# Weight tiles kept in attention's resting K and V buffers, and the first K at the head of the queue

## The chip, the cores and the metric

The kernel runs on one core of a Trainium2 chip. Times are microseconds (us) of the device. The kernel before took 807.57 us, the median of three runs (807.21 to 809.88).

The engines are named as the profile names them: PE is the matrix engine, PEld its weight loads, DVE the vector engine, ACT the scalar engine, POOL the GpSimd engine, and SP the engine whose queue starts nearly all DMAs. SPq is SP's sequencer.

## The reference

Block-sparse attention over 4 batches, 8 heads, 768 positions and 64 features, then a feed-forward layer over all 3072 positions:

```python
scores = scale * np.matmul(q, k.transpose(0, 1, 3, 2))
mask = np.abs(blk_i - blk_j) <= 1                      # blocks of 32
mask = mask | (blk_i == 0) | (blk_j == 0) | (blk_i == n_blocks - 1) | (blk_j == n_blocks - 1)
for qb in range(n_blocks):
    for kb in sampled_blocks[qb]:                      # three sampled blocks for each
        mask[qb * block:(qb + 1) * block, kb * block:(kb + 1) * block] = True
attn = softmax(np.where(mask, scores, -1e9))
x = np.matmul(attn, v)                                 # -> (3072, 512)
h = x @ w_in                                           # (512, 2048)
return (h - np.tanh(h)) @ w_out                        # (2048, 512)
```

## The kernel before, in words

**Feed-forward units.** The 3072 tokens are six chunks of 512, the 2048 hidden features sixteen stripes of 128. A unit is one chunk with one stripe `ft`; there are 96 (`UNITS`). `first` makes h of the unit by 12 matmuls with the tile `wi` of the stripe, `bent` makes h - tanh(h) on ACT, DVE and POOL, and `second`, two units later, adds the stripe's part of the output by 12 matmuls with the tile `wo`. Weights and activations are split into a high and a low part (hence three products for each). A tile `wi` or `wo` is 128x1024 words, 512 KB, high half and low half.

**The order of the units** (`SEGS`): units 0 to 7 are chunk 0 with stripes 0 to 7, units 8 to 15 chunk 1 with stripes 0 to 7, units 16 to 23 chunk 1 with stripes 8 to 15, units 24 to 31 chunk 0 with stripes 8 to 15, and from unit 32 on a chunk at a time.

**How a weight tile is made.** The weights come as 64-bit words. `load` brings the raw words of a tile (512 KB) into one of three raw buffers (two tiles `rv` and `spare`), `convert` makes 32-bit numbers of them by three operations on DVE, by way of a PSUM bank, and `split` writes the high part (ACT) and the low part (POOL). `save` writes the finished tile to device memory (`w2i`, `w2o`), from which `get` brings it back for a later chunk. Tiles of stripes 0 to 2 stay on the chip; the others pass through rings of three tiles, `wi` and `wo`. The stripes of the first half are made before and during units 0 to 7, those of the second half during units 8 to 22, one each 0.94 units (`CONVB`). Their conversion passes through PSUM banks 6 and 7, which attention also uses.

**What `ahead` means.** A second-half tile that is made more than `AHEAD` = 2.2 units before its use is split in place: high and low part are written over the raw words. It is then saved, and fetched again by `get` for its unit among 16 to 23. All sixteen are such tiles. A raw buffer is free for the next load only when the save has read it.

**Attention.** It works in attention units of their own, each with one query block and half of the heads. Attention units 0 to 7 run before feed-forward unit 0, attention units 8 to 15 (for chunk 1) until about unit 8, and attention unit 16 starts near 22.7. For each, `gather_k` copies the K blocks that its queries see into `kr0` or `kr1` (on POOL; on DVE for the first two), `gather_v` brings the V rows into `vw00`, `vw01` or `vw10`, `vw11` by DMA, `scores` multiplies, and so on. `fresh` leaves out the blocks that a buffer still holds. `load_samples` reads the sampled block numbers and computes on DVE the offsets `kx` and `vx`, which the gathers read into registers. `ks` holds all of K, half 0 and half 1, four DMAs of 768 KB each (`load_k`).

**What sets the order.** Each step is put into a list with a time in units (`at`), the list is sorted, and each engine then runs its instructions in that order, SP its DMAs too. Nothing overtakes: a DMA that must wait on SP holds those behind it.

The lines that set the second half's order are these:

```python
ahead = ft >= HALF and ft + HALF + NEED[m] - t0 > AHEAD
at(max(t0 - 1.8, free[k - 3] if k > 2 else -99), self.load, m, ft, k)
at(end + 0.03, self.split, m, ft, ahead)
at(end + 0.4, self.save, m, ft)
free.append(end + (1.2 if ahead else 0.01))
at(max(u + g, sent[m, ft]), self.get, m, u)
```

Of the kernel before, what the change touches and what calls it, by code (L numbers as in the profile page):

```python
# [11 lines left out]
F32 = mybir.dt.float32  # L12
F32R = mybir.dt.float32r
# [28 lines left out]
STEPS = dict(w=0.5, t=0.61, hs=0.605, th=0.82, p1=0.83, qq=0.87, mk=0.97, p2=1.05, p3=1.27, cp=1.49, gh=1.78, gl=1.9)  # L42
GETI, GETO = -1.6, 1.0
NEED = {"i": -0.6, "o": 1.9}
AHEAD = 2.2
CHUNKS = [[4 * n + 1 + j for j in range(4)] for n in range(5)] + [[21, 22, 0, 23]]
HALF = NFT // 2
SEGS = [(0, 0, HALF), (1, 0, HALF), (1, HALF, NFT), (0, HALF, NFT)] + [(n, 0, NFT) for n in range(2, len(CHUNKS))]
# [99 lines left out]
class Attention:  # L148
    def __init__(self, tc, k, q, v, samp, rows, ffn, ident, banks, att, sm, f2, rv, at):
        self.tc, self.nc = tc, InOrder(tc)  # L150
        self.k, self.q, self.v, self.ffn, self.ident, self.banks = k, q, v, ffn, ident, banks
        self.sm, self.f2, self.att, self.rv = sm, f2, att, rv
        self.ks = att.tile([P, 2, H, S], F32, name="ks")
        self.vw = [[att.tile([P, B, VW], F32, name=f"vw{i}{x}") for x in range(2)] for i in range(2)]
        self.kr = [att.tile([P, H, 256], F32, name=f"kr{i}") for i in range(2)]
        self.kx, self.vx = (att.tile([1, 66], I32, name=f"{n}x") for n in "kv")
        self.held = {}
        self.vals, self.qs, self.ve = {}, {}, {}
        self.ms, self.nbs, self.ps, self.pts, self.nbe, self.es, self.wts = ({} for _ in range(7))
        self.kept = [ffn.spare.bitcast(F32)[:, 256 * i : 256 * i + 256] for i in range(3)]  # L160

        units = []
        last = {}

        def add(c, time, **kw):
            u = Unit(len(units), c, time, **kw)
            u.i, u.before = c, last.get(c)
            if u.n < LEAD - 2:
                u.i, u.before = u.n % 2, units[u.n - 2] if u.n > 1 else None
            elif u.n < LEAD:  # L170
                u.before = units[u.n - 2]
            if u.b:
                last[c] = u
            units.append(u)

        for c in range(2):
            for b in CHUNKS[0]:
                add(c, 0, b=b)
        for m, blocks in list(enumerate(CHUNKS))[1:]:
            steps = [(c, dict(b=b, quick=m < 3)) for b in blocks if 0 < b < NB - 1 for c in range(2)]  # L180
            edges = [(g // 2, dict(f=g % 2, k=k)) for g in EDGES.get(m, ()) for k in range(3)]
            steps += edges
            for i, (c, kw) in enumerate(steps):
                add(c, BAND[m][0] + BAND[m][1] * (i - 2 * (m == 1)), **kw)
        lead = lambda x: (x - T0) * RATE
        at(lead(-9), self.load_q, units[0])
        for bt in range(B):
            at(lead(-8.9), self.load_k, 0, bt)
        at(lead(-8.95), self.load_samples, samp, rows)
        for c, t in ((1, lead(-2.5)),):  # L190
            for bt in range(B):
                at(t, self.load_k, c, bt)
        for u in units:
            t, n = u.t, u.n
            if u.b:
                if n:
                    at(max(t["s"] - 2.0, units[n - NQ].t["s"] + 0.01) if n >= NQ else lead(-8.95 + 0.01 * n), self.load_q, u)
                at(max(t["s"] - 1.2, u.before.t["s"] + 0.01 if u.before else lead(-3)), self.gather_k, u)
                at(max(t["s"] - 2.0, u.before.t["pv"] + 0.01 if u.before else lead(-3)), self.gather_v, u)
            else:  # L200
                if u.k == 0:
                    at(units[n - 1].t["s"] + 0.02, self.load_q, u)
                at(units[n - 2].t["pv"] + 0.02, self.load_ve, u)
            at(t["s"], self.scores, u)
            at(t["m"], self.most, u)
            at(t["e1"], self.exps, u, 1)
            at(t["e0"], self.exps, u, 0)
            at(t["turn"], self.turn, u)
            at(t["c1"], self.copy, u, 1)
            at(t["c0"], self.copy, u, 0)  # L210
            at(t["pv"], self.accum, u)
            at(t["norm"], self.norm, u)
            if u.b:
                for x in "hl":
                    at(t["norm"] + (0.1 if x == "h" else 0.15), self.put, u, x)
            elif u.k == 2:
                at(t["e0"] + 0.12, self.weigh, u)
                end = 2 * u.c + u.f in EDGES[len(CHUNKS) - 1]
                quiet = iter([t["norm"] + 0.1 + 0.08 * j for j in range(6)] if end else self.quiet(units[u.n + 1 :], t["norm"]))
                for k in range(3):  # L220
                    for s in range(1 + k):
                        at(next(quiet), self.join, u, k, s)
                for i in range(2):
                    for x in "hl":
                        at(t["norm"] + 0.65 + 0.2 * i if end else LATE + 0.5 * (2 * u.c + u.f) + 0.25 * i, self.put, u, x, i)

    def quiet(self, units, time):

        for u in range(int(time) + 1, NU):
            near = [x for v in units for x in (v.t["m"], v.t["c1"], v.t["norm"])]  # L230
            yield max((u + 0.56 + 0.04 * i for i in range(6)), key=lambda x: min([1] + [abs(x - y) for y in near]))

    def load_k(self, c, bt):
        self.nc.sync.dma_start(out=self.ks[:, c, 2 * bt : 2 * bt + 2], in_=self.k[c][:, 2 * bt : 2 * bt + 2])
# [59 lines left out]

    def gather_k(self, u):
        nc, i = self.nc, u.i
        k, to = self.ks[:, u.c], self.kr[i]
        e = nc.vector if u.n < 2 else nc.gpsimd
        for s, b, n in self.fresh(("k", i), u, self.near(u) + [(3, 0), (4, NB - 1)]):
            o = slice(32 * s, 32 * (s + n)) if s < 4 else slice(131, 256, 4)  # L300
# [3 lines left out]

    def gather_v(self, u):
        e, i = self.nc.sync, u.i
        (wa, ra), src = self.vw[i], self.v[u.c]
        near = [(s, b if 0 < b < NB - 1 else NB + 8) for s, b in self.near(u)]
        for s, b, n in self.fresh(("v", i), u, near + [(3, 0), (4, NB - 1)]):
            row = 32 * b if b < NB else S  # L310
# [14 lines left out]
    def scores(self, u):  # L325
        for h in range(2):
            for q in range(4):
                for j in range(2):
                    f, b = u.at(h, j)
                    r, i = slice(64 * j, 64 * j + 64), 4 * f + q  # L330
                    rhs = self.kr[u.i][r, i] if u.b else self.ks[r, u.c, i, 256 * u.k : 256 * u.k + 256]
                    o = self.banks[u.banks["s"][j]][32 * q : 32 * q + 32, 256 * h : 256 * h + 256]
                    self.mm(o, self.qs[u.c, b][r, i], rhs)

# [43 lines left out]
    def accum(self, u):  # L378
        o = self.banks[u.banks["o"]]
        for j in (1, 0):  # L380
            for h in range(2):
                for x in range(2):
                    for q in range(4):
                        e = slice(65 * q, 65 * q + 65)
                        t = self.pts[u.n, j][:, P * (2 * h + x) + 32 * q : P * (2 * h + x) + 32 * q + 32]
                        r = self.vw[u.i][x][:, 2 * h + j, e] if u.b else self.ve[u.n][:, x, j, e]
                        c = slice(65 * (2 * h + j), 65 * (2 * h + j) + 65)
                        self.mm(o[32 * q : 32 * q + 32, c], t, r, start=j == 1 and h == 0 and x == 0, stop=x == 1)

# [64 lines left out]
class FFN:  # L454
# [10 lines left out]
        self.x, self.w, self.h, self.work, self.raw, self.done = {}, {}, {}, {}, {}, {}  # L465

    def parts(self, m, u):
        ft = UNITS[u][1]
        if ft < KEPT:
            t = self.res[m, ft]  # L470
        else:
            t = self.wb.tile([P, 2, 512], F32R, tag=f"w{m}", name=f"w{m}{u}")
        self.w[m, u] = t[:, 0], t[:, 1]
# [18 lines left out]
            self.tmp = tmp or self.short(f"tmp{m}{ft}")  # L492
        convert_op(self.nc, self.raw[m, ft], self.work[m, ft], self.tmp, x)

    def split(self, m, ft, ahead):
        t = self.work.pop((m, ft))
        if ahead:
            to = self.raw[m, ft].bitcast(F32R)
        else:
            to = self.parts(m, UNITS.index((ft // HALF, ft)))  # L500
        hi, lo = to[:, 0:512], to[:, 512:1024]
        self.done[m, ft] = to
        self.nc.scalar.activation(out=hi, in_=t.bitcast(F32), func=AF.Copy)
# [106 lines left out]
    def plan(self, at):  # L610
        t, done = lambda x: (x - T0) * RATE, []
        banks = [x.bitcast(I32) for x in self.banks]
        halves = [sorted(((m, ft) for ft in range(a, a + HALF) for m in "io"), key=lambda w: w[1] + NEED[w[0]]) for a in (0, HALF)]
        slots = [(t(3.3 + 1.6 * k), 0.3 * RATE, None) for k in range(4)] + [(x, 0.09, banks[b]) for x, b in zip(CONVA, CONVAB)]
        slots += [(CONVB[0] + CONVB[1] * k, 0.12, banks[6 + k % 2]) for k in range(2 * HALF)]
        sent, free = {}, []
        for k, ((m, ft), (t0, dt, tmp)) in enumerate(zip(halves[0] + halves[1], slots)):
            ahead = ft >= HALF and ft + HALF + NEED[m] - t0 > AHEAD
            at(max(t0 - 1.8, free[k - 3] if k > 2 else -99), self.load, m, ft, k)
            for x in range(3):  # L620
                at(t0 + dt * x, self.convert, m, ft, x, tmp)
            end = t0 + 2 * dt
            at(end + 0.03, self.split, m, ft, ahead)
            if ft >= KEPT:
                at(end + 0.4, self.save, m, ft)
            free.append(end + (1.2 if ahead else 0.01))
            sent[m, ft] = end + 1.3
            if not ahead:
                done.append((m, UNITS.index((ft // HALF, ft))))
        self.ends = [e for e in ENDS if e != 2 * HALF]  # L630
        for u in range(NU):
            n, ft = UNITS[u]
            for m, g in (("i", GETI), ("o", GETO)):
                if ft < KEPT:
                    self.w[m, u] = tuple(self.res[m, ft][:, x] for x in range(2))
                elif (m, u) not in done:
                    at(max(u + g, sent[m, ft]), self.get, m, u)
            for c in range(NCT):
                at(u + 0.125 * c, self.first, u, c)
            for y, t in STEPS.items():  # L640
# [55 lines left out]
```

## Time and profile before

| | |
|---|---|
| median of three runs | 807.57 us |
| the profiled execution | 810.89 us |
| its span (first to last instruction) | 809.1 us |
| PE busy | 744.0 us (92%) |
| DVE busy | 546.8 us (68%) |
| ACT busy | 478.7 us (59%) |
| POOL busy | 333.9 us (41%) |
| mean granted TensorE clock | 0.986 |
| DMA traffic | 162.81 MB, mean 201 GB/s |

The shares are means over stages that differ: in the first 75 us attention runs alone, up to about 150 us the first weights are made beside the first units, up to about 250 us the second half's are made, and after that PE is busy without a break. A stage is read from the windows of the profile, the wait that holds it from the chain of waits. Nearly every operation stands under one line of the program (L79, the recorder), so operations are told by the names of what they write and read: `x<-y` is x written from y.

### The profile page before, as it was taken

How to read it: one execution, taken by the hardware profiler on the slowest of the kernel's cores; microseconds unless marked ns; L12 is line 12 of the kernel's file. 1: busy time of each engine (PE TensorE's matmuls, PEld its weight loads, DVE VectorE, ACT ScalarE, POOL GpSimd, SP SyncE). 2: the span in 40 equal slices, each digit the busy share in tenths (PEclk: the TensorE clock that was granted, in tenths of full speed). 3: DMA queues.
4: the chain of work that ended last, by engine and by line, in shares of the span. 5: the costliest groups of instructions: out<-in, count | busy, mean ns of one | idle time of the engine just before them, and what ended most of it. 6: DMA issues, size and time to landing. Idle time of an engine off the chain costs nothing.

```text
span 809.1 us, 20672 instructions
## 1 busy us (share of the span) xinstructions
PE 744.0 (92%) x8128; PEld 564.0 (70%) x8128; DVE 546.8 (68%) x970; ACT 478.7 (59%) x1021; POOL 333.9 (41%) x400
## 2 busy tenths in 40 slices
PE   0678888998878999999999999999999999999996
PEld 0456566776656777777777777777777777888885
DVE  3566876877765666677666687766676667866554
ACT  0566766665556676656555666566565655655543
POOL 2785665565656555434422234321332311212221
PEclk9889999999999999999999999999999999999998
DMA  8977754489899585465666156574337455237542
GB/s 283 324 233 222 232 211 151 156 295 332 290 333 316 180 261 175 154 188 186 221 219 190 42 163 221 174 275 149 108 106 282 132 183 198 104 83 245 193 156 78
DMA packets 56787, 162.81 MB, mean 201 GB/s; under 512 B 9331, under 2 KB 15988, under 8 KB 56692
## 3 DMA queue, kind: packets, MB, share of 16 engines
q1 hardware_dynamic: 56308, 160.98, 60.2%
q8 instruction: 64, 1.05, 0.5%
q10 hardware_dynamic: 384, 0.52, 0.2%
q14 instruction: 31, 0.25, 0.1%
HBM read 140.49 MB, written 20.97 MB: 200 GB/s over the span
## 4 chain that ended last, share of the span: by engine, by line
PE 69%; DMA 11%; DVE 10%; ACT 5%; issue 2%; SPq 1%; POOL 1%; DVEq 0%; POOLq 0%
PE ps L79 69%; DVE ps L79 5%; DMA rawi<-w 3%; DMA vw<-v 2%; DMA spare<-w 2%; DMA rawo<-w 2%; SPq L79 1%; DMA ks<-k 1%; ACT pt L79 1%; DVE m L79 1%; DVE cvto L79 1%; ACT p L79 1%; DMA w2o<-rawo 1%; DVE cvti L79 1%; DVE t L79 1%
## 5 line engine op out<-in xcount | busy, mean ns | idle before, releaser
L79 PE MATMUL ps<-x,wi 128*128 128x512 f32 x936 | 240.3, 398 | 7.1 <-DMA wi<-w2i 3.5
L79 POOL TENSOR_TENSOR gl<-t,gh 128x512 fp32r<-128x512 f32 x96 | 124.0, 1291 | 240.6 <-ACT gh L79 119.5
L79 PEld LDWEIGHTS ps<-x,wi 128*128 128x128 f32 x936 | 171.1, 188 | 53.1 <-DVE ps L79 7.8
L79 PE MATMUL ps<-wo,gh 128*128 128x512 f32 x624 | 202.3, 406 | 4.0 <-DMA wo<-w2o 4.0
L79 PEld LDWEIGHTS ps<-wo,gh 128*128 128x128 f32 x624 | 113.1, 189 | 38.6 <-issue 14.1
L79 PE MATMUL ps<-wo,gl 128*128 128x512 f32 x312 | 123.5, 397 | 1.4 <-POOL gl L79 1.4
L79 ACT ACTIVATE u<-ps 128x512 f32<-128x512 f32 x96 | 57.2, 596 | 89.3 <-PE ps L79 88.3
L79 POOL COPY kr<-ks 128x256 f32 (+2 forms) x182 | 95.3, 618 | 16.9 <-DMA vw<-v 14.8
L79 DVE TENSOR_REDUCE m<-ps 128x2 f32<-128x512 f32 x112 | 72.0, 684 | 35.3 <-PE ps L79 34.7
L79 PE MATMUL ps<-kr,q 64*32 64x256 f32 x1408 | 59.4, 401 | 27.3 <-POOL kr L79 19.0
L79 POOL TENSOR_TENSOR x<-xt,x 128x256 fp32r<-128x256 f32 (+1 forms) x48 | 34.5, 720 | 110.1 <-ACT x L79 110.0
L79 DVE TENSOR_TENSOR ps<-ps,u 128x512 f32<-128x512 f32 x96 | 66.5, 693 | 15.0 <-ACT t L79 15.0
L79 DVE COPY_PREDICATED t<-mk,ps 128x512 f32<-128x512 int32 x96 | 71.4, 744 | 7.1 <-DVE ps L79 0.5
L79 ACT ACTIVATE p<-ps,nb 128x256 f32<-128x256 f32 x176 | 73.9, 471 | 3.0
L79 DVE TENSOR_TENSOR t<-t,ps 128x512 f32<-128x512 f32 x64 | 43.7, 683 | 46.5 <-ACT t L79 46.5
L79 DVE SCALAR_TENSOR_TENSOR ps<-qq,ps 128x512 f32<-128x512 f32 x96 | 66.4, 691 | 8.3 <-ACT qq L79 2.8
L79 PEld LDWEIGHTS ps<-wo,gl 128*128 128x128 f32 x312 | 58.9, 189 | 17.2 <-POOL gl L79 3.1
L79 ACT ACTIVATE qq<-u,bias 128x512 f32<-128x512 f32 x96 | 69.5, 724 | 0.0
L79 ACT ACTIVATE mk<-u,bias 128x512 f32<-128x512 f32 x96 | 69.3, 722 | 0.0
L79 DVE SCALAR_TENSOR_TENSOR ps<-u,ps 128x512 f32<-128x512 f32 x96 | 66.4, 691 | 1.9
L79 ACT ACTIVATE pt<-ps 128x512 f32<-128x512 f32 x72 | 41.5, 598 | 42.8 <-PE ps L79 42.6
L79 PEld LDWEIGHTS ps<-vw,pt 128*32 128x32 f32 x2816 | 43.5, 111 | 30.7 <-ACT pt L79 10.2
(96 smaller groups left out, 957.2 us busy)
## 6 DMA issues: line engine op xcount, KB each, us to landing
wi<-w2i SPq DMA_DIRECT2D x73, 512.0 KB, 5.2
wo<-w2o SPq DMA_DIRECT2D x73, 512.0 KB, 4.8
vw<-v SPq DMA_DIRECT2D x182, 130.0 KB, 3.3
q<-q SPq DMA_DIRECT2D x52, 128.0 KB, 4.8
ve<-v SPq DMA_DIRECT2D x24, 260.0 KB, 4.8
ks<-k SPq DMA_DIRECT2D x8, 768.0 KB, 7.6
rawi<-w SPq DMA_DIRECT2D x11, 512.0 KB, 4.9
rawo<-w SPq DMA_DIRECT2D x11, 512.0 KB, 5.2
```

The costliest lines, as they stand in the source:

```text
L79: r = f(*args, **kw)
```

## The change

Chunk 1's units 16 to 23 take the second half's tiles straight from where `split` writes them, without a way through device memory. The tiles of stripes 8 to 11 are written into buffers lent by attention between attention units 15 and 16: `li0` to `li3` (the `wi` tiles) into `kr0` and `kr1`, two in each, `lo0` to `lo3` (the `wo` tiles) into the four `vw` buffers. Those of stripes 12 to 15 are written into the rings `wi` and `wo`. No tile is split in place any more, and a raw buffer is free when `convert` has read it. All sixteen tiles are still saved, for the chunks that use them later. Attention units 16 and 17 find nothing held in `kr` and `vw` and gather all their blocks again. The conversions of `o13` and `i15` (the tiles `wo` of stripe 13 and `wi` of stripe 15) change places, and the last split is 0.35 units later.

At the start, the four DMAs of K's first half stand ahead of the first q and of the samples.

```diff
-AHEAD = 2.2
...
-        self.vw = [[att.tile([P, B, VW], F32, name=f"vw{i}{x}") for x in range(2)] for i in range(2)]
-        self.kr = [att.tile([P, H, 256], F32, name=f"kr{i}") for i in range(2)]
+        self.vws, self.krs, self.loans = {}, {}, {}
+        ffn.lent = self.lent
...
-        at(lead(-9), self.load_q, units[0])
+        at(lead(-8.97), self.load_q, units[0])
         for bt in range(B):
-            at(lead(-8.9), self.load_k, 0, bt)
+            at(lead(-9), self.load_k, 0, bt)
         at(lead(-8.95), self.load_samples, samp, rows)
...
+    def kr(self, u):
+        key = u.i, u.n < 8 + CT * 2
+        if key not in self.krs:
+            self.krs[key] = self.att.tile([P, H, 256], F32, tag=f"kr{u.i}", name=f"kr{u.i}_{u.n}")
+            self.held.pop(("k", u.i), None)
+        return self.krs[key]
...
+    def lent(self, m, i):
+
+        if m == "o":
+            return self.att.tile([P, 1040], F32R, tag=f"vw{i // 2}{i % 2}", name=f"lo{i}")[:, 0:1024].rearrange("p (x f) -> p x f", x=2)
+        if i // 2 not in self.loans:
+            self.loans[i // 2] = self.att.tile([P, 2, 2, 512], F32R, tag=f"kr{i // 2}", name=f"li{i}")
+        return self.loans[i // 2][:, i % 2]
...
     def parts(self, m, u):
-        ft = UNITS[u][1]
+        n, ft = UNITS[u]
         if ft < KEPT:
             t = self.res[m, ft]
+        elif n == 1 and HALF <= ft < HALF + 4:
+            t = self.lent(m, ft - HALF)
         else:
...
-    def split(self, m, ft, ahead):
+    def split(self, m, ft):
         t = self.work.pop((m, ft))
-        if ahead:
-            to = self.raw[m, ft].bitcast(F32R)
-        else:
-            to = self.parts(m, UNITS.index((ft // HALF, ft)))
+        to = self.parts(m, UNITS.index((ft // HALF, ft)))
...
+        halves[1].insert(13, halves[1].pop(12))
...
-            ahead = ft >= HALF and ft + HALF + NEED[m] - t0 > AHEAD
...
-            at(end + 0.03, self.split, m, ft, ahead)
+            at(end + 0.03 + 0.35 * (k == len(slots) - 1), self.split, m, ft)
...
-            free.append(end + (1.2 if ahead else 0.01))
-            sent[m, ft] = end + 1.3
-            if not ahead:
-                done.append((m, UNITS.index((ft // HALF, ft))))
+            free.append(end + 0.01)
+            done.append((m, UNITS.index((ft // HALF, ft))))
...
-                    at(max(u + g, sent[m, ft]), self.get, m, u)
+                    at(u + g, self.get, m, u)
```

**SP's queue in the second half.** The names: `raw` and `spare` are raw loads, a row into `w2i` or `w2o` is a save, a row into `wi` or `wo` is a get, and the number behind `raw` or `w2i`, `w2o` is the stripe, behind `lo` the stripe less 8, behind `wi` and `wo` the unit; the last number only counts tiles. Before, from the raw load of stripe 12's `wo` to the save of stripe 12's:

```order
L79 DMA rawo12_2746<-w 128x1024
L79 DMA wi19_2751<-w2i11_110 128x1024
L79 DMA w2o11_123<-rawo11_2640 128x1024
L79 DMA wo17_2787<-w2o9_121 128x1024
L79 DMA rawi15_2798<-w 128x1024
L79 DMA w2i14_113<-spare_134 128x1024
L79 DMA wi20_2808<-w2i12_111 128x1024
L79 DMA wo18_2845<-w2o10_122 128x1024
L79 DMA spare_134<-w 128x1024
L79 DMA w2o12_124<-rawo12_2746 128x1024
```

Of the change, between the same two:

```order
L78 DMA rawo12_2726<-w 128x1024
L78 DMA w2o11_123<-lo3_2738 128x1024
L78 DMA rawo13_2773<-w 128x1024
L78 DMA w2i14_113<-wi22_2790 128x1024
L78 DMA spare_134<-w 128x1024
L78 DMA w2o12_124<-wo20_2837 128x1024
```

The gets are gone, one `wi` and one `wo` for each unit from 16 to 23, sixteen in all, and the saves read the tile and no longer the raw buffer.

**POOL where attention unit 16 begins.** Before:

```order
L79 TENSOR_TENSOR gl_19_2983<-t_19_2873,gh_19_2971 128x512
L79 COPY kr0_143<-ks_138 128x8x32
L268 TENSOR_LOAD kx_145
L79 ISA
L79 TENSOR_TENSOR rawo14_2909<-cvto14_3014,rawo14_2909 128x512
L79 TENSOR_TENSOR t_21_3047<-t_21_3047,hs_21_3045 128x512
L79 TENSOR_TENSOR gl_20_3074<-t_20_2931,gh_20_3059 128x512
```

Of the change:

```order
L78 TENSOR_TENSOR gl_19_2980<-t_19_2865,gh_19_2967 128x512
L78 COPY kr0_16_3007<-ks_138 128x8x64
L78 COPY kr0_16_3007<-ks_138 128x8x32 x3
L289 TENSOR_LOAD kx_139
L78 ISA
L78 COPY kr0_16_3007<-ks_138 128x8x32
L78 TENSOR_TENSOR wo22_3052<-cvto14_3005,wo22_3052 128x512
L78 TENSOR_TENSOR t_21_3042<-t_21_3042,hs_21_3040 128x512
L78 TENSOR_TENSOR gl_20_3075<-t_20_2920,gh_20_3055 128x512
```

Behind each `ISA`, a register's load, stands one copy of a sampled block, three in both kernels (repeated rows are left out here). Ahead of them one copy of 32 columns has become one of 64 and three of 32. The same holds for `kr1` and attention unit 17.

**SP at the start.** Before:

```order
L79 DMA q0_1_147<-q 128x256
L79 DMA room_149<-samp 1x144
L79 DMA room_149<-rows 1x66
L79 DMA q1_2_169<-q 128x256
L79 DMA q2_3_171<-q 128x256
L79 DMA q3_4_173<-q 128x256
L79 DMA ks_138<-k 128x1536 x4
L79 DMA vw00_139<-v 32x1040
```

Of the change:

```order
L78 DMA ks_138<-k 128x1536 x4
L78 DMA q0_1_145<-q 128x256
L78 DMA room_147<-samp 1x144
L78 DMA room_147<-rows 1x66
L78 DMA q1_2_167<-q 128x256
L78 DMA q2_3_169<-q 128x256
L78 DMA q3_4_171<-q 128x256
L78 DMA vw00_0_173<-v 32x1040
```

The four K loads now stand ahead of the samples and of four q loads, which DVE's offsets and the gathers need.

## Rows read from the trace of the kernel before

**Rows 1.** Windows of 25 us: busy us of PE, PEld, DVE, ACT, POOL, clock, DMA.
```profile
150.00:175.00 25.00, 23.57 (x101) 18.30 (x100) 20.20 (x32) 17.52 (x32) 16.93 (x14) 1.00 0.71 251
...
225.00:250.00 25.00, 18.13 (x94) 12.63 (x99) 16.15 (x24) 11.87 (x22) 14.73 (x17) 1.00 0.99 335
250.00:275.00 25.00, 25.00 (x307) 19.20 (x290) 15.85 (x29) 18.13 (x41) 14.52 (x18) 1.00 0.79 263
```

**Rows 2.** The chain that ended last, in order of time: start, us, what.
```profile
17.53 9.48 DMA ks<-k
...
181.01 4.92 DMA rawi<-w
...
214.76 6.09 DMA w2o<-rawo
220.90 4.24 DMA rawi<-w
...
240.43 6.21 DMA rawo<-w
```

**Rows 3.** Timeline of SP's queue, 150 to 260 us: start, us, instruction, count.
```profile
214.32 0.39 SPq L79 DMA_DIRECT2D wi<-w2i  x1
...
215.28 0.38 SPq L79 DMA_DIRECT2D wo<-w2o  x1
```

**Rows 4.** Timeline of PE; in brackets the idle time before and its releaser.
```profile
160.83 2.91 PE L79 MATMUL ps<-x,wri 128*128 128x512 f32 x12
...
166.38 2.91 PE L79 MATMUL ps<-x,wi 128*128 128x512 f32 x12
...
178.28 2.91 PE L79 MATMUL ps<-x,wi 128*128 128x512 f32 x12
182.37 0.70 PE L79 MATMUL ps<-wo,gh 128*128 128x512 f32 x2 [1.18 <-DMA wo<-w2o]
...
241.77 2.98 PE L79 MATMUL ps<-x,wi 128*128 128x512 f32 x12 [1.40 <-DMA wi<-w2i]
...
249.35 1.09 PE L79 MATMUL ps<-kr,q 64*32 64x256 f32 x30 [2.37 <-DVE cvto L79]
```

**Rows 5.** DMA in the window 150 to 250 us.
```profile
DMA packets 8739, 29.75 MB, mean 297 GB/s; under 512 B 1045, under 2 KB 1301, under 8 KB 8733
```

**Rows 6.** Timeline of DVE, the first of the steps of `bent` in four units.
```profile
173.19 0.70 DVE L79 TENSOR_TENSOR ps<-ps,u 128x512 f32<-128x512 f32 x1 [1.49 <-ACT t L79]
...
179.29 0.70 DVE L79 TENSOR_TENSOR ps<-ps,u 128x512 f32<-128x512 f32 x1 [1.50 <-ACT t L79]
...
185.12 0.70 DVE L79 TENSOR_TENSOR ps<-ps,u 128x512 f32<-128x512 f32 x1 [1.49 <-ACT t L79]
...
190.72 0.70 DVE L79 TENSOR_TENSOR ps<-ps,u 128x512 f32<-128x512 f32 x1 [0.66 <-ACT t L79]
```

**Rows 7.** Timeline of POOL, from the lead and from where attention unit 16 begins.
```profile
45.85 2.47 POOL L79 COPY kr<-ks 128x512 f32<-128x512 f32 x4
...
237.38 1.98 POOL L79 COPY kr<-ks 128x256 f32<-128x256 f32 x4
241.41 1.28 POOL L79 TENSOR_TENSOR rawo<-cvto,rawo 128x512 fp32r<-128x512 f32 x1 [2.04 <-ACT rawo L79]
```

**Rows 8.** Timeline of the start, SP, DVE and PE.
```profile
2.85 0.18 DVE L79 CAST room<-room 1x66 f32<-1x66 int32 x1 [1.94 <-DMA room<-samp]
...
3.19 2.13 SPq L79 DMA_DIRECT2D ks<-k  x4
...
6.08 0.18 DVE L79 TENSOR_SCALAR kx<-room 1x66 int32<-1x66 f32 x1
...
16.05 2.06 SPq L79 DMA_DIRECT2D ks<-k  x4
16.11 4.79 DVE L79 COPY kr<-ks 128x768 f32<-128x768 f32 x7 [9.85 <-DMA vw<-v]
...
18.61 1.96 PE L79 MATMUL ps<-kr,q 64*32 64x256 f32 x32 [18.61 <-POOL kr L79]
```

More of the change, by code (lines that the diff above doesn't have):

```diff
@@ L231, in quiet, with vw @@
             yield max((u + 0.56 + 0.04 * i for i in range(6)), key=lambda x: min([1] + [abs(x - y) for y in near]))
+    def kr(self, u):
[4 more added lines that the diff above has]
+        return self.krs[key]
+    def vw(self, u):
+        key = u.i, u.n < 8 + CT * 2
+        if key not in self.vws:
+            self.vws[key] = [self.att.tile([P, B, VW], F32, tag=f"vw{u.i}{x}", name=f"vw{u.i}{x}_{u.n}") for x in range(2)]
+            self.held.pop(("v", u.i), None)
+        return self.vws[key]
+    def lent(self, m, i):
[4 more added lines that the diff above has]
+        return self.loans[i // 2][:, i % 2]
     def load_k(self, c, bt):
@@ L296, in gather_k @@
         nc, i = self.nc, u.i
-        k, to = self.ks[:, u.c], self.kr[i]
+        k, to = self.ks[:, u.c], self.kr(u)
         e = nc.vector if u.n < 2 else nc.gpsimd
@@ L306, in gather_v @@
         e, i = self.nc.sync, u.i
-        (wa, ra), src = self.vw[i], self.v[u.c]
+        (wa, ra), src = self.vw(u), self.v[u.c]
         near = [(s, b if 0 < b < NB - 1 else NB + 8) for s, b in self.near(u)]
@@ L330, in scores @@
                     r, i = slice(64 * j, 64 * j + 64), 4 * f + q
-                    rhs = self.kr[u.i][r, i] if u.b else self.ks[r, u.c, i, 256 * u.k : 256 * u.k + 256]
+                    rhs = self.kr(u)[r, i] if u.b else self.ks[r, u.c, i, 256 * u.k : 256 * u.k + 256]
                     o = self.banks[u.banks["s"][j]][32 * q : 32 * q + 32, 256 * h : 256 * h + 256]
@@ L385, in accum @@
                         t = self.pts[u.n, j][:, P * (2 * h + x) + 32 * q : P * (2 * h + x) + 32 * q + 32]
-                        r = self.vw[u.i][x][:, 2 * h + j, e] if u.b else self.ve[u.n][:, x, j, e]
+                        r = self.vw(u)[x][:, 2 * h + j, e] if u.b else self.ve[u.n][:, x, j, e]
                         c = slice(65 * (2 * h + j), 65 * (2 * h + j) + 65)
@@ L613, in plan @@
         halves = [sorted(((m, ft) for ft in range(a, a + HALF) for m in "io"), key=lambda w: w[1] + NEED[w[0]]) for a in (0, HALF)]
+        halves[1].insert(13, halves[1].pop(12))
         slots = [(t(3.3 + 1.6 * k), 0.3 * RATE, None) for k in range(4)] + [(x, 0.09, banks[b]) for x, b in zip(CONVA, CONVAB)]
         slots += [(CONVB[0] + CONVB[1] * k, 0.12, banks[6 + k % 2]) for k in range(2 * HALF)]
-        sent, free = {}, []
+        free = []
         for k, ((m, ft), (t0, dt, tmp)) in enumerate(zip(halves[0] + halves[1], slots)):
-            ahead = ft >= HALF and ft + HALF + NEED[m] - t0 > AHEAD
             at(max(t0 - 1.8, free[k - 3] if k > 2 else -99), self.load, m, ft, k)
```

## The prediction, made before the changed kernel ran

> **What bounds the kernel now.** I read the windows first, then the chain of waits where PE has holes, then the queue whose DMAs stand in that chain, last PE's and DVE's own order there. In the windows the reader is to see two stages: up to 250 us PE is busy for 23.57 of 25 us at 150 and for only 18.13 at 225, while the DMA engines' share climbs from 0.71 to 0.99; from 250 us on PE is busy for all of 25.00 [rows 1]. So time lost before 250 us is lost for good, and time won there is kept, since PE alone paces what follows. The chain says whose holes these are: from 181 to 247 us it goes through DMAs, mostly raw loads, of 4.24 to 6.21 us each, ten pieces with some DVE work between them; rows 2 has four of these pieces. One turn can be read off whole: a save issued at 214.76 takes 6.09 us, and at 220.90 the next raw load starts [rows 2]. It had to, since that load writes the buffer that the save reads. Between the two SP also issued a get of `wi` and one of `wo` [rows 3], so each turn puts four transfers of 512 KB into one queue, and the load stands behind all of them.
>
> What the stage loses is counted on PE. Unit 10's first product starts at 160.83, unit 11's at 166.38 [rows 4]: 5.55 us for 24 matmuls with no wait worth naming. A turn of DVE's loop with PE full, 185.12 to 190.72, is 5.60 [rows 6], and I take that as a unit's price. Counting the groups of 12 first products onward, unit 13 starts at 178.28 and unit 22 at 241.77 [rows 4]: nine units in 63.49 us, where nine at 5.6 are 50.4. Waits for a get (1.18 at 182.37, 1.40 at 241.77) are part of these 13.1 us. Then attention unit 16's scores wait another 2.37 us for the conversion of the last `wo` tile [rows 4], whose raw load was issued at 240.43 and took 6.21 us [rows 2].
>
> **The change, part by part.**
>
> *Sixteen gets go.* They are 16 x 512 KB = 8.4 MB of the 29.75 MB that the window of 150 to 250 us moves at 297 GB/s [rows 5], 28 us of the queue at that rate. The refill of the `vw` buffers gives back 2 x 128 rows of 4160 bytes, 1.1 MB. What is left, 22.4 MB, needs 75 us at 297 GB/s, and the stage will last about 85. The queue then has slack, though not in units 11 to 14, where the gets for the first half's stripes stay beside loads and saves.
>
> *Raw loads no longer wait for saves.* A load now waits only until DVE has converted the tile three before it, and it stands in SP's order 1.8 units, some 10 us, ahead of its conversion. A load takes 4.24 to 6.21 us [rows 2], so it lands with 4 us to spare. Nearest to late are the `wo` gets for units 11 to 15: each stands behind a save that waits for POOL. From the order I get 1.5 to 3 us to spare for each.
>
> *What is late next.* With transfers on time, PE's 5.6 us and DVE's loop remain. In units 11 to 13 the loop is longer: the first step of `bent` starts at 173.19, 179.29 and 185.12, each time after 1.5 us of waiting for ACT's `t`, 6.1 and 5.8 apart. In the next turn it is 5.6 (190.72) and the wait is 0.66 [rows 6]. The reason stands in the times of the list: conversions come each 0.94 units, so each stands 0.06 units earlier against its unit than the one before; by then the conversion no longer ends just ahead of ACT's split, and the split no longer holds up `u`, `hs` and `t`. That shift is the same in the changed kernel. I charge 0.5 us for unit 13, and 5.6 for the units from 14 on. Gain up to unit 22: 63.49 - 50.9 = 12.6 us. With the conversion on time the 2.37 us go too. Together 15.0.
>
> *In-order waits that stay.* The window 150 to 175 us, where DMA is not yet full, still has PE idle for 1.43 of 25 us [rows 1], 6%. Over nine units that would be 3 us; most of it comes from the longer loop already charged. I take 1.0, between 0 and 3.
>
> *The refill of `kr`.* Each of two attention units adds three copies of 32 columns to POOL and makes one of them 64 wide. Four copies of 32 columns took 1.98 us, four with a wide one 2.47 [rows 7], so 0.5 for the widening and 1.5 for three more: 2.0 us for each unit. Ahead of unit 21's product on POOL stand eight copies (4 us) and a low half (1.28 us [rows 7]). POOL needs three operations of 1.28 us each unit, 3.9 of 5.6 us, so 4 us more in two units does not fit at once. Laid out on POOL's order, `gl` of unit 20 ends some 1.6 us after PE wants it; unit 21's is on time again. Before, POOL waited 2.04 us for late tiles just there [rows 7], which hid such work. I charge 1.6, between 0 and 4 (all of it).
>
> *The refill of `vw`* lands 2 to 3 units ahead of its use, and the loans' last readers are done by then but for `lo3`, which SP may await for a few tenths. Nothing urgent stands behind it. 0.
>
> *New waits of the split.* Tiles of stripes 12 to 15 now go into ring slots that PE must have left. In the list's units each slot is free 0.7 units or more ahead, but for the last, `o15`, which is why it moved by 0.35. ACT's next work there waits for PE anyway. 0, at most 1. That the saves stay costs nothing on the path: nobody waits for their buffers.
>
> *First K at the head.* Before, the K loads are issued at 3.19 and the copies from K start at 16.11 [rows 8]; the four DMAs move up by 2.4 us. But the sample words, which DVE got at 2.85 and turned into `kx` by 6.08 + 0.18 us [rows 8], now stand behind 3 MB of K. If they land just after K (10.5 to 13.5 us), `kx` comes 3.4 us later, at 14 to 17, and the copies, which stand behind that work on DVE, at 14 to 17 as well, against 16.11. And the chain does not go by the first K but by the second: issued from 16.05, its last piece at 17.53 landing 9.48 us later [rows 2, 8]. Those loads stand on SP behind three gathers that need `vx`, which comes with `kx`: they start at 16 to 18, into an emptier queue. I take 0; -2 to +2.5.
>
> The Trainium skill (DMA: Bandwidth & Descriptors, section Queues, rings and completion order) says that each DMA engine takes its descriptors in the order of its ring. By that rule the samples can't pass K, and the copies gain 2 us at best; if small transfers did pass, they could start near 13 us and gain 3. No run so far shows a small transfer behind a large one on this queue, so this is open.
>
> **The sum.** 15.0 - 1.0 - 1.6 = 12.4 us. The profiled execution took 810.89 us, so it would be 798.5 for one like it; that execution lay 3.3 above the median of the three runs, 807.57, which becomes 795.2.
>
> **The rivals.**
>
> 1. *The DVE and ACT loop stays long.* Every unit from 13 to 21 then costs 6.1 us, as at 173 to 179, not 5.6: 9 x 0.5 less the 1.5 charged is 3 us lost, gain 9.4, time 798. For it: PE is only 94% busy where DMA was not full. Against it: the turn of 5.6 us at 190.72 while conversions ran on [rows 6].
>
> 2. *The samples come late.* K lands at 13.5, the samples behind it, the second K is issued 2.5 to 4 us later and the whole lead moves with it: gain 8.5 to 10, time 798. For it: the chain runs through the second K [rows 2]. Against: DMAs that stood in its way before are then done.
>
> 3. *It does nothing that shows*: the stage is paced by loads, saves and the remaining gets as it was, and PE waits for `wi` and `wo` now and then as before. Only the 2.37 us go, and POOL's refill takes 1.6 of these: 806.8. Against it: after unit 16 two transfers are left for each unit where four were.
>
> 4. *Slower: ACT is held at the ring.* Each of the eight splits into a ring waits on ACT, in order, for PE's last reader of the slot; PE waits for ACT's `gh`; each such turn costs a PE group, 2.8 us or so with its restart. From 1.55 us a tile (12.4 / 8) the gain is eaten; at 2 us each it is 811. For it: before, the splits waited for no reader, and PE's order leads ACT's by little at `o15`. Against: 0.7 units, 4 us, to spare for seven of the eight.
>
> **How the numbers follow.** My forecast, 795.2, gets 0.60, with a range of its own from 792 to 798 by the bounds of the 1.0, the 1.6 and the start. Rival 1 gets 0.17, rival 2 0.09, rival 3 0.06, rival 4 0.08. About 0.3% (2.4 us) is what a measurement tells from no change. Faster by more than that are the first three, 0.86; within it rival 3, 0.06; slower 0.08. The range for 8 in 10 takes in the forecast with its bounds and rivals 1 and 2 with theirs: from 791 (all costs at their low end, the start 2 us better) to 803 (the loop long and the samples late together, 802, with a part of POOL's bound).
>
> **What would show it.** Right: in the windows from 175 us to the start of attention unit 16 PE busy for 24 us or more of 25 and DMA well below 0.9; units 14 to 21 at 5.6 to 5.8 us between first products; no raw load in the chain there; the scores of attention unit 16 near 235 us; one wait for `gl` of 1 to 2 us just ahead of it. From there to the end the same length as before. Wrong: raw loads still in the chain; units at 6.1 (rival 1); the second K issued after 18.5 us (rival 2); PE or ACT waiting for each other at a split into `wi` or `wo` (rival 4).

## The result, and the profile after

The changed kernel takes 795.23 us, the median of four runs (794.40 to 797.82), against 808.55 for the kernel before, the median of the four runs beside it (807.21 to 809.88). The ratio is 0.9841 (95%: 0.981 to 0.9871). The forecast was 795.2, and the mechanism was the one it named; two of its terms were mis-sized, in opposite directions.

The profiled execution of the change took 797.82 us, with a span of 796.1, 13.0 less than the span before. The first products of three units on PE cut these 13.0 us into stages. The timeline of PE, 150 to 250 us, of the changed kernel (start, us, instruction, count, in brackets the idle time before and its releaser):

```profile
179.96 2.91 PE L78 MATMUL ps<-x,wi 128*128 128x512 f32 x12
...
186.07 2.91 PE L78 MATMUL ps<-x,wi 128*128 128x512 f32 x12
...
219.80 2.89 PE L78 MATMUL ps<-x,wi 128*128 128x512 f32 x12
223.49 0.50 PE L78 MATMUL ps<-lo,gl 128*128 128x512 f32 x1 [0.33 <-POOL gl L78]
...
225.90 2.90 PE L78 MATMUL ps<-x,wi 128*128 128x512 f32 x12
...
231.42 2.92 PE L78 MATMUL ps<-x,wi 128*128 128x512 f32 x12
...
235.27 0.50 PE L78 MATMUL ps<-wo,gl 128*128 128x512 f32 x1 [0.47 <-POOL gl L78]
...
236.40 1.09 PE L78 MATMUL ps<-kr,q 64*32 64x256 f32 x32
...
238.93 2.90 PE L78 MATMUL ps<-x,wi 128*128 128x512 f32 x12
```

Units 13, 22 and 23 start at 179.96, 231.42 and 238.93. Before, units 13 and 22 started at 178.28 and 241.77 [rows 4], and unit 23 at 251.88. So up to unit 13 the change lost 1.7 us, from there to unit 22 it won 12.0 (51.5 where 63.5 stood), from 22 to 23 another 2.6 (7.5 where 10.1 stood), and from unit 23 to the end nothing (557.2 us in both): 12.0 + 2.6 - 1.7 is 12.9 of the 13.0. From unit 13 to the scores of attention unit 16 at 236.40, which wait for nothing, no DMA ends a wait of PE. What is left are short waits for `gl`, POOL's product.

The windows of the same execution (25 us each, columns as in rows 1) show the stage full:

```profile
175.00:200.00 25.00, 24.39 (x104) 18.95 (x103) 20.25 (x32) 16.92 (x31) 17.74 (x14) 1.00 0.91 320
200.00:225.00 25.00, 24.67 (x107) 19.55 (x106) 23.01 (x36) 18.58 (x34) 17.45 (x15) 1.00 0.68 234
225.00:250.00 25.00, 24.53 (x223) 18.62 (x222) 17.96 (x30) 17.16 (x37) 22.51 (x30) 1.00 0.81 250
```

The last of these answers to the 18.13 us of PE and the 0.99 of DMA in [rows 1]: PE is busy for 24.53 us, and the DMA engines have slack. In the first window they have little: 0.91, where the prediction's sign was well below 0.9. In the chain that ended last, where raw loads stood before [rows 2], PE itself now stands:

```profile
183.63 5.81 PE ps L78 x24
189.47 27.75 PE ps L78 x118
...
228.21 2.79 POOL kr L78 x6
...
235.27 24.84 PE ps L78 x311
```

The same shows on SP, in what it waited for in the whole program (us in total, times, longest). Before:

```profile
SPq L79 <- DMA w2o<-rawo: 19.6, 5, 5.2
SPq L79 <- DMA w2i<-rawi: 15.6, 3, 5.8
...
SPq L79 <- DMA w2i<-spare: 9.7, 3, 4.1
...
SPq L79 <- DMA w2o<-spare: 6.1, 2, 4.6
```

SP stood for 51.0 us behind saves that had not landed. In the change no save stands in this list.

The pieces of POOL from 228 to 235 us in the chain, seven copies into `kr` with the tile half, `t` and `gl` behind them, hold the refill's price. The wait of 0.33 us for `gl` at 223.49 comes before any refill copy. POOL's timeline:

```profile
228.14 3.40 POOL L78 COPY kr<-ks 128x512 f32<-128x512 f32 x7
...
233.89 1.33 POOL L78 TENSOR_TENSOR gl<-t,gh 128x512 fp32r<-128x512 f32 x1
```

Seven copies take 3.40 us where four took 1.98 [rows 7]. The `gl` behind them ends at 235.22, and PE waited 0.47 us for it.

At the start, SP, DVE and PE of the change:

```profile
10.97 0.18 DVE L78 CAST room<-room 1x66 f32<-1x66 int32 x1 [10.05 <-DMA room<-samp]
...
14.43 2.46 DVE L78 COPY kr<-ks 128x768 f32<-128x768 f32 x7
...
17.19 2.23 SPq L78 DMA_DIRECT2D ks<-k  x4
...
17.92 3.67 PE L78 MATMUL ps<-kr,q 64*32 64x256 f32 x64 [17.92 <-POOL kr L78]
```

The sample words reach DVE at 10.97, not 2.85; the copies start 1.7 us earlier, PE 0.7 earlier, and the second K is issued 1.1 us later than in [rows 8].

### The profile page after: what moved, and what is told of

Read it like the earlier page. It is cut to its first block, busy times and chain, and to the rows that moved or that the text cites. A ratio compares the mean times of both kernels' runs of the same rounds, so it can differ in the third digit from the quotient of the medians.

```text
span 796.1 us, 20648 instructions
## 1 busy us (share of the span) xinstructions
PE 742.5 (93%) x8128; PEld 564.5 (71%) x8128; DVE 544.1 (68%) x970; ACT 478.0 (60%) x1021; POOL 335.0 (42%) x406
## 4 chain that ended last, share of the span: by engine, by line
PE 75%; DVE 9%; ACT 5%; DMA 4%; POOL 3%; issue 2%; SPq 1%; POOLq 0%; DVEq 0%
PE ps L78 75%; DVE ps L78 4%; DMA vw<-v 2%; ACT pt L78 1%; SPq L78 1%; ACT p L78 1%; DMA ks<-k 1%; DMA room<-rows 1%; DVE m L78 1%; POOL gl L78 1%; DVE cvto L78 1%; POOL kr L78 1%; DVE cvti L78 1%; POOL t L78 1%; DVE t L78 1%
## 5 line engine op out<-in xcount | busy, mean ns | idle before, releaser
L78 PE MATMUL ps<-x,wi 128*128 128x512 f32 x888 | 228.3, 398 | 0.0
L78 PEld LDWEIGHTS ps<-x,wi 128*128 128x128 f32 x888 | 162.5, 188 | 42.4 <-issue 7.4
L78 PE MATMUL ps<-wo,gh 128*128 128x512 f32 x592 | 190.9, 404 | 0.0
L78 PEld LDWEIGHTS ps<-wo,gh 128*128 128x128 f32 x592 | 107.0, 188 | 30.9 <-issue 7.4
L78 PE MATMUL ps<-wo,gl 128*128 128x512 f32 x296 | 117.0, 397 | 2.8 <-POOL gl L78 2.8
L78 PEld LDWEIGHTS ps<-wo,gl 128*128 128x128 f32 x296 | 55.6, 188 | 18.4 <-POOL gl L78 5.3
```

The lines of the kernel that those rows point to most:

```text
L78: r = f(*args, **kw)
```

## The experiments

Each was timed in five rounds beside the kernel before on the same chip (medians of the kernel before: 809.0, 808.9 and 807.07 in the three groups). Two questions were open: what the start costs, and whether the stage was held by the wait of the raw load for the save, or by the traffic of the gets.

### The start: each half alone

`e1_old_start` is the change with q and samples ahead of the first K, as before:

```diff
-        at(lead(-8.97), self.load_q, units[0])
+        at(lead(-9), self.load_q, units[0])
-            at(lead(-9), self.load_k, 0, bt)
+            at(lead(-8.9), self.load_k, 0, bt)
```

> The change with the start of before (q, samples, three q, then K); all else as changed. Ring theory: with K first the sample words wait behind 3 MB of K (they reached DVE at 10.97 instead of 2.85 us), so kx, vx and the second K come late (its first load was issued at 17.19 instead of 16.05) and the lead is 1 to 2 us longer; this kernel is then 1 to 2 us faster than the changed one, 793 to 794, the second K issued near 16.05. Clock theory: the 1.7 us that the profiled execution of the change lost up to unit 13 are its lower clock in 25 to 75 us (0.80 against 0.86) and have nothing to do with the order: then this kernel takes 795, within 0.5 us of the change.

Measured: 792.95 us, ratio 0.9801 (0.9776 to 0.9826), about what the ring theory gave. `e2_k_first_alone` is the kernel before with the opposite edit and no loans:

> The kernel before with nothing but K's first half put ahead of q and the samples. Ring theory: 1 to 2 us slower than before, the second K issued near 17.2 us. Clock theory: within 0.5 us of before. If the earlier K gave anything (the copies from K start 1.7 us sooner), it would be 1 to 2 us faster.

Measured: 811.17 us, ratio 1.0027 (1.0006 to 1.0048). So the change without its new start is worth some 16 us, and the first K at the head costs about 2.2. To see both on one chip, the change and its old start ran again (`e9_change_again`, `e10_old_start_again`, no new edit):

> The changed kernel once more, as it is. If its start (first K at the head) costs 2.2 us, as adding it to the kernel before did, this is 795 us, and the same kernel with the old start beside it on this chip 793. If that 2.2 was chance or belongs only to the kernel before, both are alike within 0.5 us, near 794.

> The change with the old start, as in e1_old_start: 793 us, some 2 below the change beside it, if the start costs 2.2; within 0.5 us of it otherwise.

Measured: 795.94 (794.67 to 798.19, six runs, ratio 0.9854, 0.9819 to 0.9889) and 793.58 (791.41 to 795.17, six runs, ratio 0.9818, 0.9783 to 0.9853). The intervals of the ratios overlap, but the 2.4 us between the medians are near the 2.2 of `e2_k_first_alone`. The profiled executions say the same: in the four kernels with the change's start (the two of the change, `e5_gets_as_traffic` and `e7_refill_early` below) unit 13 begins at 178.44 to 180.25, in the three with the loans and the old start (`e1_old_start`, `e10_old_start_again`, `e11_refill_on_dve`) at 176.24 to 178.03, on average 2.2 us earlier. The kernel with the loans and the old start is the best version found.

The windows of the first 30 us show where it may go (columns as in rows 1). The change:

```profile
0.00:14.00 14.00, 0.00 (x0) 0.00 (x0) 2.65 (x17) 1.28 (x1) 0.70 (x6) 1.00 0.84 308
14.00:18.00 4.00, 0.08 (x8) 0.08 (x16) 2.86 (x10) 0.00 (x0) 2.16 (x4) 1.00 0.25 77
18.00:30.00 12.00, 9.94 (x208) 5.64 (x208) 4.98 (x10) 8.11 (x23) 6.71 (x13) 1.00 0.99 339
```

The change with the old start, `e10_old_start_again`:

```profile
0.00:14.00 14.00, 0.00 (x0) 0.00 (x0) 3.06 (x19) 1.28 (x1) 0.70 (x6) 1.00 0.81 283
14.00:18.00 4.00, 0.00 (x0) 0.00 (x0) 2.11 (x4) 0.00 (x0) 2.07 (x3) 1.00 0.93 256
18.00:30.00 12.00, 10.39 (x216) 6.04 (x216) 7.53 (x14) 7.87 (x23) 9.90 (x18) 1.00 1.02 360
```

With K at the head the queue is nearly empty from 14 to 18 us (77 GB/s), because the gathers need `vx`, `vx` needs the sample words, and these came at 10.97. With the old start it moves 256 GB/s. The 4 us x 179 GB/s, 0.7 MB, are not lost whole, since with K at the head the queue had moved 0.35 MB more by 14 us. But the three windows together make 8.7 MB by 30 us, where the old start has 9.3. The 0.6 MB are about 1.8 us at the 340 to 360 GB/s of the last window: near the size of the loss, as an estimate.

### The start: can both come early?

`e3_samples_first` puts the samples first, then K, then q. `e4_samples_on_act` keeps the change's order but starts the two sample loads from ACT's queue:

```diff
-        at(lead(-8.95), self.load_samples, samp, rows)
+        at(lead(-9.05), self.load_samples, samp, rows)
```
```diff
-        self.nc.sync.dma_start(out=si, in_=samp)
-        self.nc.sync.dma_start(out=ri, in_=rows)
+        self.nc.scalar.dma_start(out=si, in_=samp)
+        self.nc.scalar.dma_start(out=ri, in_=rows)
```

> The change, with the two small sample loads ahead of the K loads, which stay ahead of q. Ring theory: the samples land near 2.9 us, K 0.8 us later than in the change, near 11.6; the copies from K start there and no longer at 14.4, the second K is issued near 14 instead of 17.2 and the lead is 2 to 4 us shorter than in the change: 791 to 793. Clock theory: no more than 0.5 us from the change, 795.

> The change, with the two sample loads issued from ACT's queue and not from SP's. If the samples wait in the ring of SP's own queue, they land near 3 to 4 us from another queue though K is under way, kx is there before K, and the time is that of the kernel with the samples ahead of K on SP, 791 to 793. If they wait for the DMA engines themselves, whatever the queue, they land near 11 us again and the time stays at 795.

Measured: 794.67 (0.9817, 0.9793 to 0.984) and 794.75 (0.9823, 0.9799 to 0.9848): both miss. DVE, PE and SP of `e3_samples_first`:

```profile
2.01 0.18 DVE L78 CAST room<-room 1x66 f32<-1x66 int32 x1 [1.09 <-DMA room<-samp]
...
14.05 1.96 PE L78 MATMUL ps<-kr,q 64*32 64x256 f32 x32 [14.05 <-POOL kr L78]
...
5.79 9.50 SPq L78 DMA_DIRECT2D vw<-v  x7
15.34 2.21 SPq L78 DMA_DIRECT2D ks<-k  x4
...
28.30 0.35 SPq L78 DMA_DIRECT2D rawi<-w  x1
```

DVE of `e4_samples_on_act`:

```profile
2.08 0.18 DVE L78 CAST room<-room 1x66 f32<-1x66 int32 x1 [1.17 <-DMA room<-samp]
5.22 0.47 DVE L78 TENSOR_TENSOR room<-room 1x66 f32<-1x66 f32 x2 [2.95 <-DMA room<-rows]
```

Both did what was meant: the sample words are there at 2 us (the second list, `rows`, at 5.22 from ACT's queue) and PE's scores start near 14, some 4 us earlier than in the change. But in `e3_samples_first` the seven V gathers hold SP for 9.50 us, the second K leaves at 15.34, and the first raw load at 28.30, hardly before the 28.79 of the change and after the 27.03 of the kernel before. In `e4_samples_on_act` the raw load leaves at 27.84. An earlier first score was not what the lead needed.

`e8_second_k_early` asks whether the second K's place on SP is what counts: old start, and the second K right behind the first.

```diff
-        for c, t in ((1, lead(-2.5)),):
+        for c, t in ((1, lead(-3.05)),):
```

> The change with the start of before, and K's second half put ahead of the V gathers of attention units 0 and 1, right behind K's first half. If the second K's landing sets the lead (the first raw weight load waits for it on SP), it lands near 20 to 21 us and no longer at 25.5 to 29, the raw load is issued 3 us or more earlier, and the time is 2 to 4 us under that of the change with the old start: 789 to 791. If the DMA queue as a whole sets the lead, the V rows come later by what K comes earlier, and the time stays at 793.

Measured: 794.89 (0.9845, 0.9816 to 0.9873), above both expectations. SP's timeline there:

```profile
3.19 4.33 SPq L78 DMA_DIRECT2D ks<-k  x8
7.98 19.28 SPq L78 DMA_DIRECT2D vw<-v  x14
27.30 0.59 SPq L78 DMA_DIRECT2D rawi<-w  x1
```

The second K leaves SP by 7.5 us, some 10 us sooner, and the gathers behind it take the time instead: the raw load leaves at 27.30. By 30 us the kernels of `e3_samples_first`, `e4_samples_on_act` and this run had moved 9.1 to 9.3 MB, nearly as much as with the old start, and their profiled executions begin unit 13 at 177.04 to 177.67, within the range of the old start; their medians, 794.7 to 794.9, still lie between those of the change and of the old start. So neither the first score nor the second K's place sets the lead by itself. That the lead is as long as the queue's transfers, and that a hole in it is paid for, fits these runs, but no run changed the hole alone: the cause of the 2.2 us is argued, not shown.

### The stage: wait or traffic

`e6_gets_left_out` is the kernel before without the sixteen gets of units 16 to 23, which multiply with stripe 0's tiles instead (so those units' share of the output is another). The loads still wait for the saves:

```diff
+                elif 2 * HALF <= u < 3 * HALF:
+                    self.w[m, u] = tuple(self.res[m, 0][:, x] for x in range(2))
```

> The kernel before (tiles split in place, raw loads waiting for the saves, K behind the samples) without the sixteen gets: units 16 to 23 use the kept weights of stripe 0 in their place, so the output is wrong there. Traffic theory: with the queue relieved the saves land in 3 to 4 us and not 6, raw loads are on time, and nearly all the 14.6 us are won: 793 to 796. Wait theory: load, conversion, split and save still follow each other on each raw buffer, the raw loads stay in the chain and units cost over 6 us: 800 to 805.

Measured: 801.67 (0.9927, 0.99 to 0.9953). ACT's first step of units 13 and 22 stands 55.5 us apart, where it was 61.3 before and 49.1 in the change: about half of the 12 us goes with the traffic, half stays with the wait. The time lies in the range of the wait theory. The chain there, and SP's waits for saves in the whole program:

```profile
202.57 5.55 DMA w2i<-rawi
...
208.18 4.30 DMA rawo<-w
```
```profile
SPq L79 <- DMA w2o<-rawo: 17.2, 4, 4.8
...
SPq L79 <- DMA w2i<-rawi: 14.4, 3, 5.1
SPq L79 <- DMA w2i<-spare: 11.4, 3, 4.8
...
SPq L79 <- DMA w2o<-spare: 4.4, 2, 4.1
```

A save of 5.55 us, then the raw load: with the gets gone the loads still stand in the chain behind saves, and SP still stands behind saves for 47.4 us, where it was 51.0.

`e5_gets_as_traffic` is the reverse: the change, with sixteen copies of finished tiles within device memory on SP where the gets were, which nobody waits for.

```diff
+    def dump(self, m, u):
+        ft = UNITS[u][1]
+        self.nc.sync.dma_start(out=self.dumps[m, ft], in_=self.two[m, ft])
...
+                elif u >= 2 * HALF:
+                    at(max(u + g, sent[m, ft]), self.dump, m, u)
```

> The change, with the sixteen gets of units 16 to 23 put back as traffic alone: at each get's place SP copies the same 512 KB of w2 to a part of device memory that nobody reads; the units still use the tiles kept on the chip, and raw loads still wait for no save. If the 8.4 MB of traffic were what held the stage, 175 to 250 us must carry what it did before at about 300 GB/s and most of the 12 us go again: 804 to 808. If the raw loads' wait for the saves was what held it, there are buffers enough in advance and the time stays near the change: 795 to 798.

Measured: 800.07 (0.9893, 0.9863 to 0.9923), between the two. The profile divides it. One window, and PE and SP behind the stage:

```profile
200.00:225.00 25.00, 24.66 (x107) 19.83 (x106) 23.06 (x36) 19.48 (x36) 18.23 (x15) 1.00 1.02 396
```
```profile
249.71 4.51 PE L78 MATMUL ps<-x,wi 128*128 128x512 f32 x12 [2.51 <-DMA wi<-w2i]
...
242.68 0.43 SPq L78 DMA_DIRECT2D wi<-w2i  x1
```

In the stage the DMA engines are full (1.02, 396 GB/s, where the kernel before moved 285 in this window) and PE is as busy as without the copies; units 13 to 22 take 49.0 us by ACT's first step, as in the change (49.1). The 4.4 us that the profiled execution lost lie behind unit 23: a get that chunk 0 needs was issued at 242.68 behind two of the copies and a save, PE waited 2.51 us for it, and the next twelve products took 4.51 us instead of 2.9. That the copies made this get late was not tested by itself. So traffic costs the stage nothing once no load waits for a save; what was lost came with the first get behind it, a late transfer of another kind. Together the two runs say how the effects combine: the gets make each turn of save and load longer, and the turn matters only because the load waits.

### The refill of `kr`

`e7_refill_early` issues the fixed copies of attention units 16 and 17 about 1.7 units earlier on POOL:

```diff
+                if n in (16, 17):
+                    at(19.95 + 0.95 * (n - 16), self.gather_k, u, 0)
```

> The change, with the fixed copies of attention units 16 and 17 into kr (one of 64 columns, three of 32) moved on POOL by about 1.7 units to earlier places; the sampled blocks' copies stay. By the prediction's 1.6 us for the refill: 793 to 794. By the profile of the change, where PE waits 0.33 and 0.47 us for gl in units 21 and 22: 0.5 us at most, so 795.

Measured: 796.41 (0.986, 0.983 to 0.989): neither expectation came. PE there:

```profile
230.79 0.51 PE L78 MATMUL ps<-lo,gl 128*128 128x512 f32 x1 [1.45 <-POOL gl L78]
233.23 2.93 PE L78 MATMUL ps<-x,wi 128*128 128x512 f32 x12
240.01 2.90 PE L78 MATMUL ps<-x,wi 128*128 128x512 f32 x12
```

Units 22 to 23 take 6.78 us instead of 7.51, with the wait of 0.47 gone: 0.7 is what the refill cost there, the wait and PE's slower restart after it. But the wait turned up a unit earlier as 1.45, ahead of unit 22. POOL has this work to do in either place.

`e11_refill_on_dve` gives the fixed copies to DVE (with the old start):

```diff
-        e = nc.vector if u.n < 2 else nc.gpsimd
+        e = nc.vector if u.n < 2 or u.n in (16, 17) else nc.gpsimd
```

> The change with the old start, and the fixed blocks of kr (one copy of 64 columns, three of 32) of attention units 16 and 17 copied by DVE, not POOL. If POOL's refill costs 0.5 us, as the wait of 0.47 for gl ahead of attention unit 16 says, that wait goes, nothing else moves, and the time is 792.5. If the prediction's 1.6 were right, 791.4. If DVE is the tighter engine there (its loop is 5.6 us of work a unit in the prediction), the 2 us of copies come ahead of the conversion and of m, and the time is 794 to 795.

Measured: 801.09 (797.41 to 803.18; 0.9905, 0.9871 to 0.994), 7.5 us above `e10_old_start_again` on the same chip: the direction that the expectation gave for a tight DVE, but three times its size or more. PE and DVE, then a window of PE with its clock:

```profile
234.33 0.50 PE L78 MATMUL ps<-wo,gl 128*128 128x512 f32 x1 [1.64 <-POOL gl L78]
...
238.42 1.96 PE L78 MATMUL ps<-kr,q 64*32 64x256 f32 x30 [2.35 <-DVE cvto L78]
...
225.94 2.50 DVE L78 COPY kr<-ks 128x512 f32<-128x512 f32 x4
...
234.31 3.53 DVE L78 COPY kr<-ks 128x512 f32<-128x512 f32 x4
237.69 0.67 DVE L78 SCALAR_TENSOR_TENSOR cvto<-rawo,ps 128x512 int32<-128x512 int32 x1
```
```profile
238.00:241.00 3.00, 2.58 (x32) 1.27 (x33) 0.90 (x2) 0.00 (x0) 0.88 (x1) 0.50 0.05 17
```

The copies stand ahead of `cvto` on DVE and push the last conversion to 237.69; the scores of attention unit 16 wait 2.35 us for it, which is the wait of [rows 4] come back. The first four copies delay the conversion before it, so POOL's `gl` is later, not earlier (1.64). And behind the two waits the granted clock was 0.50 (1.2 GHz): the 30 scores take 1.96 us, where 32 took 1.09. From unit 22 (229.30) to unit 23 (243.03) PE took 13.7 us, 6.2 more than in `e10_old_start_again`; 3.5 of these are the longer waits, and the scores and products around them at the lower clock are the rest. The other 1.3 of the 7.5 were not traced.

## Why the prediction was right, point by point

*What bounded the stage.* Right. The turn of save and raw load held it, and its removal gives PE back 12 us. `e6_gets_left_out` shows that taking out the gets alone gives half of that, and `e5_gets_as_traffic` that taking out the wait alone gives all of it in the stage. No run left out the exchange of `o13` and `i15` and the later last split, so their part is not known. The prediction named both parts without dividing them.

*Units 13 to 22.* 50.9 was charged, and 1.0 for in-order waits; it is 51.5. Unit 13 took 6.1, as charged. Unit 14 took 5.8, where 5.6 was charged, and unit 20 took 6.1, with a wait of 0.33 for `gl`; the other six are at 5.5 to 5.8. Rival 1, the loop at 6.1 in every unit, did not come.

*The 2.37 us of attention unit 16.* Gone, as said. With the refill in it the step from unit 22 to 23 is 2.6 shorter.

*The refill of `kr`.* The step that failed in size. The prediction laid out POOL's order and let `gl` of unit 20 end 1.6 us after PE wants it. It counted eight copies there; the order has seven. They took 3.40 us, not the 4.0 reckoned, but `gl` came only 0.47 late, and the price is 0.7 us (`e7_refill_early`). The widened copies were inside a stretch in which POOL had had 2.04 us to spare [rows 7]; the prediction named that cover and charged as if little of it remained.

*The first K.* Taken as 0, between -2 and +2.5; the paired kernels say a loss of 2.2 to 2.4, near the far end of the range. The steps were right one by one: `kx` after 14 us, the second K issued at 17.19. The step that failed is "into an emptier queue", written down as a relief. The queue was nearly empty from 14 to 18 us because the gathers could not be issued, and by 30 us it was 0.6 MB behind the old start. That this hole is the loss is the likeliest reading, not a shown one. Rival 2 named the late samples and the late second K, with the second K 2.5 to 4 us later (it was 1.1), and it came together with the forecast's gain, not in its place.

*What the sample words do.* The prediction left open whether small transfers pass large ones on this queue. Here they did not: DVE had the sample words at 10.97 us behind 3 MB of K on SP, and at 2.08 us from ACT's queue with the same K under way. That agrees with the Trainium skill (DMA: Bandwidth & Descriptors, section Queues, rings and completion order), by which each queue row has a ring of its own on each DMA engine, and an engine turns from row to row. The second list, issued on ACT's queue too, kept DVE waiting until 5.22; no run shows why.

*Rivals 3 and 4.* Neither came. No wait of PE ends at a split, and raw loads have left the chain.

The forecast of 795.2 for a measured 795.23 owes something to chance. It was reckoned from the 807.57 us of three runs; beside the change the kernel before had a median of 808.55, so the gain was 13.3 us by these and not 12.4, and 11.1 when both ran again. And the terms cancel: the refill cost 0.9 us less than charged and the in-order waits 0.4 less, the conversion's step gave 0.9 more (2.6 and the refill's 0.7, less 2.37; most of it stands in the scores, which the wait before had cut into 2 and 30 matmuls of 0.62 and 1.09 us, where all 32 now take 1.09), and the start took 2.2 us that were not charged.

The single profile is no measure of the start. Its loss up to unit 13 was 1.7 us in the first profiled execution of the change and 0.2 in the second (unit 13 at 178.44 in `e9_change_again`); the granted clock of 25 to 75 us was 0.80 in the one and 0.86 in the other. Only several executions settle a term of 2 us there. Why the lead of one kernel varies by that much stays open.

## What to carry to other kernels

A buffer that is free only when a save has read it puts two transfers in a row into the turn of a pipeline. If the saved data can be finished in another buffer that rests, the wait goes, and the traffic around it may then cost nothing. Test which of the two it is before cutting traffic. When loads are put in front, ask what the words behind them release: here the order that let the queue run dry for 4 us cost 2.2 us, although the first consumer started earlier.

## What the runs showed of the hardware

Copies into `kr` on DVE and POOL at once were slow on both. At the start DVE's seven copies took 4.79 us in the kernel before [rows 8], where POOL copied from 16.15 us on beside them, and 2.46 in the change, where POOL began 1.4 us after DVE. In `e11_refill_on_dve` the four fixed copies took 2.50 and 3.53 us on DVE, and the three sampled copies 2.15 and 2.12 us on POOL, where `e7_refill_early`, with no copies on DVE beside them, had 1.65 and 1.64 for these three.

PE's clock did not answer to the length of a single wait alone. After the 2.37 us of the kernel before [rows 4] the scores ran at a granted clock of 1.00 (30 in 1.09 us). After waits of 1.64 and 2.35 us within 6 us the clock was at 0.50, and it was at 0.50 from 249.7 to 252 us after the 2.51 us of `e5_gets_as_traffic`, where twelve products took 4.51 us, not 2.9. With what follows it such a wait cost about 1.75 times its length: 4.4 us for 2.51, and 6.2 for the 3.5 by which the waits of `e11_refill_on_dve` grew.
